# A first MLP product by seven block products: a linear-attention and MLP kernel on one Trainium2 core

## The chip, the cores and the metric

The kernel runs on one core of a Trainium2 chip. The metric is the device time in microseconds of one execution; a time is given as the median of several runs. Lower is better. The engines are named as in the profile: PE is TensorE's matmul stream and PEld its weight loads, DVE is VectorE, ACT is ScalarE, POOL is GpSimd, SP is SyncE, whose queue issues most DMAs.

## The reference

A gated linear attention (batch 4, 8 heads, 768 tokens, head dimension 48) feeds a two-layer MLP with an ELU between the layers (3072 tokens, model dimension 384, hidden dimension 2048).

```python
f = 1.0 / (1.0 + np.exp(-f_logit))
for t in range(S):
    state = f[:, :, t, :, None] * state + np.einsum('bhd,bhe->bhde', k[:, :, t], v[:, :, t])
    y[:, :, t] = np.einsum('bhd,bhde->bhe', q[:, :, t], state)
x = y.transpose(0, 2, 1, 3).reshape(B * S, H * D)
h = x @ w_in
g = np.where(h > 0.0, h, np.exp(np.minimum(h, 0.0)) - 1.0)
out = g @ w_out
```

All tensors that the kernel computes with are fp32. The weights arrive in a wider type and are converted at the start.

## The kernel before

The 3072 tokens are cut into 12 units of 256 tokens (`NU`, `U`). For every unit the kernel runs the attention, which leaves the unit's MLP input in a tile `xt` with channels on the partitions: three channel tiles of 128 (`NKT`), and a fourth (`HP` is 4) that is only a source from which six small DMAs fill the remaining rows (L699). The MLP of a unit is cut into eight block pairs j of 256 hidden channels (`NP`). A pair P = (unit m, j) goes through these stages:

- `up(P)`: the first product, h = w_in-block transposed times `xt`, as two halves of 128 hidden channels by 256 tokens in one PSUM bank (tag `h`, two banks). Each half is three matmuls of 256 columns, one for each channel tile (L780). ScalarE then computes Relu(-h) and Exp of its negative (L785, L786).
- `elu(P)`: VectorE joins both to the ELU (L792), and for units from 2 on (`DIRECT`) forms four sums of 128x128 blocks of it (L802).
- `down(P)`: the second product. For units 0 and 1 it is four matmuls of 384 columns (L813). From unit 2 on it already is a product by seven block products of 192 columns (L835), in the manner of Strassen and Winograd: the sums of `elu` and four combinations of the w_out blocks (`combos`, made by `combine`) take the place of the eighth. After the last pair of a unit ScalarE and VectorE put the output together from four PSUM banks (L845, L846).

The attention of a unit runs in pieces: `load` (DMAs of q, k, f and v), `gates` (four ScalarE instructions and small GpSimd ones), `decays` four times (a scan and a reciprocal on VectorE at L576 and L579, products with k and q on GpSimd at L580 and L583), `transposed` (TensorE transposes, L598), `advance` (state updates on TensorE, L650), `step` (two VectorE instructions for each of four chunks, L613 and L616), `scores` and `mask` (L629, L637), `outputs` (L666) and `carried` (L686, then the copies into `xt`, L693 and L695, and the six DMAs).

The order on every engine is the order in which the code is written, under a manual schedule. The main loop counts steps T: at an even T it issues `up(T/2)`, at an odd one `down` of the pair two before (`LAG`), and ahead of them whatever `at_step` has planned for T. The attention of unit u is planned around t = (u-1)*16, one unit ahead of its MLP: `load` at t-16, `gates` at t-8, the four `decays` at t-6 to t, and the rest at t+2 to t+10. `reread` and `check` bring the weights in once more and reduce them to their smallest and largest magnitude on VectorE (L551); `finish_flag` turns this and the gates' range (`watch`) into a flag. If the flag is bad, a slower general version runs afterwards; it does not run here.

Of the kernel before, what the change touches and what calls it, by code (L numbers as in the profile page):

```python
# [8 lines left out]
FP32 = mybir.dt.float32  # L9
# [347 lines left out]
def fast(ctx: ExitStack, tc: tile.TileContext, q, k, v, f_logit, w_in, w_out, out, flag):  # L357
# [11 lines left out]

    nc = tc.nc
    B, H, D, S = q.shape
    DM = H * D
# [14 lines left out]
    DIRECT = 2  # L389
    LAG = 2  # L390
    AHEAD = 7
    LIMIT = 2.0**60
    HALF = (slice(0, D), slice(64, 64 + D))
    FULL = (slice(0, 64), slice(64, 128))
# [3 lines left out]
    sb = ctx.enter_context(tc.tile_pool(name="sb", bufs=2))  # L398
    ps = ctx.enter_context(tc.tile_pool(name="ps", bufs=1, space=bass.MemoryType.PSUM))

    NB = 3
    qkf = [{n: cst.tile([128, HP, U], FP32, name=f"{n}{i}") for n in "fqk"} for i in range(NB)]
    src = {"q": q, "k": k, "f": f_logit}
    vs = [cst.tile([128, NW, DM + PAD], FP32, name=f"v{i}") for i in range(NB)]
# [66 lines left out]
        area[:, 0:4].bitcast(FP32).rearrange("p a f -> p (a f)").rearrange("p (c n f) -> p c n f", c=4, f=DH)  # L471
    )


    both = (0, 1, 2, 3, 4, 5, 8, 9, 10, 6, 11, 7, 12, 13, 14, 15)
    order = [divmod(i, NP) for i in both] + [(m, j) for m in range(2, NU) for j in range(NP)]
# [58 lines left out]

    spans = cst.tile([128, 2, NFT], FP32, name="spans")

    def reread(n):  # L540

        if wide:
            flat = (w_out if n % 2 else w_in).rearrange("a b -> (a b)").rearrange("(p i f) -> i p f", p=128, f=2 * DM)
            nc.sync.dma_start(out=area[:, 4 + n % (AHEAD - 4)], in_=flat[n // 2])

    def check(n):

        if not wide:
            return
        for i, op in enumerate((ALU.min, ALU.max)):  # L550
            nc.vector.tensor_reduce(  # L551
                out=spans[:, i, n : n + 1], in_=area[:, 4 + n % (AHEAD - 4)].bitcast(FP32)[:, 1::2],
                axis=mybir.AxisListType.X, op=op, apply_absolute_value=True,
            )

    def gates(u, pieces=(2, 2)):
# [118 lines left out]
    def carried(u):  # L675

        t = qkf[u % NB]
        py = pys.pop(u)
        for w in range(NW):
            for p in range(HP):  # L680
                for b in range(2):
                    c = 2 * w + b
                    if (u % UPB, c) == (0, 0):
                        continue
                    for r in range(2):
                        nc.tensor.matmul(  # L686
                            py[b][HALF[r ^ b], w, p], lhsT=sts[u, c][HALF[r], p],
                            rhs=t["q"][HALF[r], p, c * C : (c + 1) * C],
                            start=False, stop=True, skip_group_check=True,
                        )  # L690
        x = xts[u] = sb.tile([128, HP, U], FP32, tag="xt", name=f"xt{u}", bufs=3)
        to = x[:].rearrange("n p (w b i) -> n b w p i", b=2, i=C)
        nc.scalar.copy(to[:, 0], py[0][:])  # L693
        for r in range(2):
            nc.scalar.copy(to[FULL[r], 1], py[1][FULL[1 - r]])  # L695
        for i in range(2 * NKT):
            r, j = divmod(i, NKT)
            frm, g = 64 * r + j * PAD, 64 * r + D
            nc.sync.dma_start(out=x[g : g + PAD, j, :], in_=x[frm : frm + PAD, NKT, :])  # L699

    def first_outputs(part):


        q_, at = qkf[0]["q"], ats[0]
        for gap in range(2):
            for w in range(NW):
                for p in range(NKT):
                    for r in range(2):
                        h = 2 * p + r
                        for b in range(2):  # L710
                            c = 2 * w + b
                            if part and c == 0:
                                continue
                            pair = NKT if gap else p
                            if part:
                                lhs = padded_s[HALF[r], c - 1, p] if gap else sts[0, c][HALF[r], p]
# [13 lines left out]
        if part == 0:  # L730
            for b in range(2):
                nc.scalar.copy(between[:, :, 0:NKT], first_y[b][:, :, :, 0])
            return
        x = xts[0] = sb.tile([128, HP, U], FP32, tag="xt", name="xt0", bufs=3)
# [7 lines left out]
    def at_step(step, *todo):  # L742
        plan.setdefault(step, []).extend(todo)

    def attention(u, first, then):

        kept = []
        for p, i in enumerate(first):
            at_step(i, lambda p=p: decays(u, p))
        if first:  # L750
            at_step(first[-1], lambda: watch(u))
        at_step(then[0], lambda: transposed(u, 0, "a0"), lambda: transposed(u, 1, "a1"))
        at_step(then[1], lambda: advance(u), *(lambda c=c: step(u, c) for c in range(NC)))
        at_step(then[2], lambda: kept.append(scores(u)))
        at_step(then[2], lambda: mask(u, kept[0]))
        at_step(then[3], lambda: outputs(u))
        at_step(then[4], lambda: carried(u))

    gs, ss, pms, phs = {}, {}, {}, {}

    def combine():
# [3 lines left out]
        for n in range(0, NP, 2):  # L765
            for to, x, y in (
# [4 lines left out]
                )  # L771
                yield

    def up(P):

        m, j = order[P]
        ph = ps.tile([128, 2, U], FP32, tag="h", name=f"psH{m}_{j}", bufs=2)
        for i in range(2):
            for kt in range(NKT):
                nc.tensor.matmul(  # L780
                    ph[:, i], lhsT=wi[j][:, kt, i * 128 : (i + 1) * 128], rhs=xts[m][:, kt, :],
                    start=(kt == 0), stop=(kt == NKT - 1),
                )
        g = gs[P] = sb.tile([128, 2, U], FP32, tag="gg", name=f"gg{m}_{j}", bufs=4)
        nc.scalar.activation(g[:], ph[:], AF.Relu, scale=-1.0)  # L785
        nc.scalar.activation(g[:], g[:], AF.Exp, scale=-1.0)  # L786
        phs[P] = ph

    def elu(P):
        m, j = order[P]  # L790
        g = gs[P]
        nc.vector.scalar_tensor_tensor(  # L792
            out=g[:], in0=g[:], scalar=-1.0, in1=phs.pop(P)[:], op0=ALU.add, op1=ALU.max
        )
        if m >= DIRECT:
            s = ss[P] = sb.tile([128, 4, 128], FP32, tag="sums", name=f"sums{m}_{j}", bufs=3)
            a = [[g[:, i, t * 128 : (t + 1) * 128] for i in range(2)] for t in range(2)]
            for i, x, y, op in (
                (0, a[1][0], a[1][1], ALU.add), (2, a[0][0], a[1][0], ALU.subtract),
                (1, s[:, 0], a[0][0], ALU.subtract), (3, a[0][1], s[:, 1], ALU.subtract),  # L800
            ):
                nc.vector.tensor_tensor(out=s[:, i], in0=x, in1=y, op=op)  # L802

    def down(P):
        m, j = order[P]
# [51 lines left out]
                    )  # L857
            del pms[m]

    def finish_flag():  # L860
        if wide:
# [7 lines left out]
        low = cst.tile([128, 1], FP32, name="low")  # L869
        nc.vector.tensor_reduce(  # L870
            out=low[:], in_=fine[:].rearrange("p a c -> p (a c)"), axis=mybir.AxisListType.X, op=ALU.min
        )
# [51 lines left out]
    decays(1, 1)  # L924
    step(0, NC - 1)
    watch(0)
    blank(2, nc.gpsimd)
    at_step(0, lambda: decays(1, 2))
    at_step(1, lambda: decays(1, 3), lambda: watch(1))
    at_step(4, lambda: warm(4))  # L930
    attention(1, (), (2, 4, 5, 6, 7))
    for n in range(1, NFT):
        t = max(needs[n][0] - 2, 0)
        at_step(t, lambda n=n: merge(n))
# [4 lines left out]
    attention(2, (14, 16, 18, 20), (22, 24, 26, 27, 28))  # L939
    weights = combine()  # L940
    for n in range(NFT):
        at_step(28 + n, lambda: next(weights))
    for u in range(3, NU):
        t = (u - 1) * NFT
        at_step(t - 16, lambda u=u: load(u))
        at_step(t - 8, lambda u=u: gates(u))
        attention(u, (t - 6, t - 4, t - 2, t), (t + 2, t + 4, t + 6, t + 8, t + 10))
    for n in range(NFT):
        t = (3 + n) * NFT + 9 if n < 7 else (NU - 2) * NFT + 9 + 2 * (n - 7) if n < 10 else (NU - 1) * NFT + 2 * n - 20
        at_step(t - 6, lambda n=n: reread(n))  # L950
        at_step(t, lambda n=n: check(n))
    at_step((NU - 1) * NFT + 13, lambda: finish_flag())
    for T in range(NU * NFT):
        P = T // 2
        if T % 2 == 0 and P:
            elu(P - 1)
        for f in plan.pop(T, ()):
            f()
# [54 lines left out]
```

## Time and profile before

| | before |
|---|---|
| median of 9 runs | 587.11 us (585.44 to 590.57) |
| the profiled execution | 586.22 us |
| its span, first to last instruction | 584.4 us |
| granted TensorE clock | 0.988 |
| PE busy / matmul instructions | 567.8 us / 5596 |
| DVE busy | 398.1 us |
| ACT busy | 217.6 us |
| POOL busy | 79.0 us |
| DMA traffic | 50.81 MB, mean 87 GB/s |

The profile is of one execution. A "busy" time is the union of an engine's instructions; their mean duration can be longer than their spacing, because matmuls are pipelined. An fp32 matmul of the program shows as two MATMUL and two LDWEIGHTS records. Groups are given as line, engine, operation, output and inputs, shape and count, then busy time and the mean duration in ns. Timeline rows give start and length in microseconds, then the same fields.

### The profile page before, as it was taken

To read this page: it belongs to the slowest core of one execution; us is meant where nothing else is said; L and a number is where in the kernel's file an instruction comes from. 1 tells how busy PE (TensorE), PEld (TensorE's weight loads), DVE (VectorE), ACT (ScalarE), POOL (GpSimd) and SP (SyncE) were. 2 spreads that over 40 slices of the span, in tenths; PEclk is the share of its full clock that TensorE was granted. 3 is DMA by queue.
4 is the path that set the end of the run, shared out by engine and by line. 5 is a ranking of instruction groups with operands and counts; after the bars stand their busy time and mean duration, and the time that the engine had idled before them with its cause. 6 is when DMAs were issued, how large, how long until landed. Compare 5 with 4: busy or idle time off the path is not lost.

```text
span 584.4 us, 13417 instructions
## 1 busy us (share of the span) xinstructions
PE 567.8 (97%) x5596; PEld 492.9 (84%) x5596; DVE 398.1 (68%) x806; ACT 217.6 (37%) x357; POOL 79.0 (14%) x161
## 2 busy tenths in 40 slices
PE   7699999999999999999999999999999999999995
PEld 2467777777899999999999899999899999999995
DVE  7899667666586676576676776766766767665852
ACT  3367845433433332432433333243252242232221
POOL 6350021020020020020021011011011011000000
PEclk9889999999999999999999999999999999999998
DMA  8999880061071061051042043034024010305401
GB/s 189 237 221 273 182 206 0 2 124 47 2 161 33 6 157 38 4 117 63 21 94 82 22 77 95 29 61 110 29 52 118 29 45 19 136 17 208 136 2 33
DMA packets 34823, 50.81 MB, mean 87 GB/s; under 512 B 4000, under 2 KB 27584, under 8 KB 34752
## 3 DMA queue, kind: packets, MB, share of 16 engines
q1 hardware_dynamic: 33840, 49.07, 33.6%
q8 instruction: 46, 0.75, 0.6%
q10 hardware_dynamic: 912, 0.79, 0.5%
q14 instruction: 25, 0.20, 0.1%
HBM read 44.04 MB, written 4.72 MB: 83 GB/s over the span
## 4 chain that ended last, share of the span: by engine, by line
PE 95%; issue 1%; POOL 1%; DMA 1%; ACT 1%; DVE 0%; DVEq 0%; POOLq 0%; ACTq 0%
PE psH L780 44%; PE psM L835 31%; PE psM L813 7%; PE psS L629 2%; PE psY L666 2%; PE psU_a L650 2%; PE psY L686 2%; PE psW L881 2%; PE psT L598 2%; PE psY L725 1%; DMA f<-in_f_logit_dram 1%; POOL k L580 0%; ACT f L564 0%; DVE at L637 0%; ACT f L563 0%
## 5 line engine op out<-in xcount | busy, mean ns | idle before, releaser
L780 PE MATMUL psH<-xt,wi 128*128 128x256 f32 x1152 | 269.3, 383 | 0.0
L780 PEld LDWEIGHTS psH<-xt,wi 128*128 128x128 f32 x1152 | 214.2, 190 | 31.4 <-issue 1.0
L785 ACT ACTIVATE gg<-psH 128x512 f32<-128x512 f32 x96 | 57.5, 599 | 268.8 <-PE psH L780 268.6
L792 DVE SCALAR_TENSOR_TENSOR gg<-gg,psH 128x512 f32<-128x512 f32 x96 | 65.8, 685 | 109.4 <-ACT gg L786 109.3
L835 PE MATMUL psM<-area,sums 128*128 128x192 f32 x480 | 91.1, 326 | 0.0
L579 DVE RECIPROCAL p<-f 128x256 f32<-128x256 f32 x48 | 84.1, 1753 | 1.7
L835 PEld LDWEIGHTS psM<-area,sums 128*128 128x128 f32 x480 | 80.2, 190 | 0.0
L835 PE MATMUL psM<-wo,gg 128*128 128x192 f32 x320 | 65.2, 326 | 0.0
L786 ACT ACTIVATE gg<-gg 128x512 f32<-128x512 f32 x96 | 60.5, 630 | 3.1
L835 PEld LDWEIGHTS psM<-wo,gg 128*128 128x128 f32 x320 | 56.3, 190 | 4.0
L580 POOL TENSOR_TENSOR k<-k,f 128x256 f32<-128x256 f32 x48 | 35.5, 741 | 166.5 <-DVE f L576 163.3
L813 PE MATMUL psM<-wo,gg 128*128 128x384 f32 x128 | 44.2, 488 | 0.0
L802 DVE TENSOR_TENSOR sums<-gg 128x128 f32<-128x128 f32 x160 | 39.4, 287 | 2.8
L835 PE MATMUL psM<-area,gg 128*128 128x192 f32 x160 | 39.1, 326 | 0.0
L835 PE MATMUL psM<-wo,sums 128*128 128x192 f32 x160 | 39.1, 326 | 0.0
L845 DVE TENSOR_TENSOR o<-psM,u 128x192 f32<-128x192 f32 (+1 forms) x30 | 11.8, 420 | 38.4 <-ACT u L846 38.1
L566 POOL COPY restart<-f 128x8 f32<-128x8 f32 (+1 forms) x24 | 4.8, 200 | 243.8 <-ACT f L564 240.2
L813 PEld LDWEIGHTS psM<-wo,gg 128*128 128x128 f32 x128 | 24.1, 190 | 13.6
L525 ACT ACTIVATE area<-area 128x768 uint16<-128x768 uint32 x16 | 30.4, 1934 | 4.7 <-DVE area L519 2.3
L576 DVE TENSOR_TENSOR_SCAN f<-f,restart 128x256 f32<-128x256 f32 x47 | 31.9, 680 | 0.0
L551 DVE TENSOR_REDUCE spans<-area 128x1 f32<-128x768 f32 x32 | 28.9, 944 | 0.0
L835 PEld LDWEIGHTS psM<-area,gg 128*128 128x128 f32 x160 | 28.2, 190 | 0.0
(82 smaller groups left out, 461.9 us busy)
## 6 DMA issues: line engine op xcount, KB each, us to landing
area<-in_moe_w_out_dram SPq DMA_DIRECT2D x16, 768.0 KB, 7.3
area<-in_moe_w_in_dram SPq DMA_DIRECT2D x8, 768.0 KB, 6.5
v<-in_v_dram SPq DMA_DIRECT2D x12, 384.0 KB, 6.8
area<-in_moe_w_in_dram SPq DMA_DIRECT2D x16, 288.0 KB, 8.3
f<-in_f_logit_dram SPq DMA_DIRECT2D x23, 192.0 KB, 3.8
k<-in_k_dram SPq DMA_DIRECT2D x23, 192.0 KB, 4.9
q<-in_q_dram SPq DMA_DIRECT2D x23, 192.0 KB, 6.0
out_dram<-o SPq DMA_DIRECT2D x38, 96.0 KB, 1.7
```

The source lines that it names most:

```text
L525: nc.scalar.activation(raw.bitcast(U16)[:, 2::4], raw.bitcast(U32)[:, 0::2], AF.Copy, scale=2.0**-29)
L551: nc.vector.tensor_reduce(out=spans[:, i, n : n + 1], in_=area[:, 4 + n % (AHEAD - 4)].bitcast(FP32)[:, 1::2], axis=mybir.AxisListType.X, ...
L576: nc.vector.tensor_tensor_scan(out=a, data0=a, data1=restart[:, p] if u or p else a, initial=1.0, op0=ALU.mult, op1=ALU.max)
L579: nc.vector.reciprocal(pts[u][:, p], g)
L580: nc.gpsimd.tensor_tensor(out=t["k"][:, p], in0=t["k"][:, p], in1=g, op=ALU.mult)
L780: nc.tensor.matmul(ph[:, i], lhsT=wi[j][:, kt, i * 128 : (i + 1) * 128], rhs=xts[m][:, kt, :], start=(kt == 0), stop=(kt == NKT - 1),)
L785: nc.scalar.activation(g[:], ph[:], AF.Relu, scale=-1.0)
L786: nc.scalar.activation(g[:], g[:], AF.Exp, scale=-1.0)
L792: nc.vector.scalar_tensor_tensor(out=g[:], in0=g[:], scalar=-1.0, in1=phs.pop(P)[:], op0=ALU.add, op1=ALU.max)
L802: nc.vector.tensor_tensor(out=s[:, i], in0=x, in1=y, op=op)
L813: nc.tensor.matmul(pm[t][:], lhsT=g[:, i, t * 128 : (t + 1) * 128], rhs=wo[:, 2 * j + i, :], start=(j == 0 and i == 0), stop=(j == NP - 1 ...
L835: nc.tensor.matmul(pm[bank][:, half * DH : (half + 1) * DH], lhsT=x, rhs=y, start=first, stop=(j == NP - 1), skip_group_check=True,)
```

## The change

From unit 2 on the first product is also computed by block products. Over the first two channel tiles, two 128-channel halves and two 128-token halves, seven products of 128x128 blocks replace eight; the third channel tile is added into three of them by matmuls into the same PSUM blocks. This takes ten matmuls, nine of 128 columns and one of 256, in two PSUM banks `pa` and `pb` of the tag `h`. Block combinations of w_in are made once on GpSimd (`mix`, in the part of `area` that the weights no longer use), those of `xt` once a unit on GpSimd (`blend`), with `xt` one tile longer. ScalarE copies one block (`u1`), VectorE adds the blocks into an SBUF tile `hh` (`up7`, `joined`), and ScalarE's two passes then read `hh` (`exped`). The four sums of `elu` move from VectorE to GpSimd, and `elu(P-1)` is issued between the two halves of `up7(P)`.

Around this, the attention's pieces get new steps (`A1`, `D2`, `A2`, `D3`, `A3`), `step` gets a slot of its own behind `advance`, q, k, f and v have two buffers instead of three (one blanking goes), the weights are reread in 32 smaller pieces into the tile `bits`, four steps apart from unit 3 to unit 10, and `finish_flag` is split in two.

```diff
+    A1 = (2, 4, 4, 5, 6, 7)
+    D2 = (14, 16, 18, 20)
+    A2 = (22, 24, 24, 26, 27, 28)
+    D3 = (-7, -5, -3, -1)
+    A3 = (2, 4, 5, 7, 9, 11)
+    BL = 13
+    RR = 0
+    MX = 21
...
-    NB = 3
+    NB = 2
...
+    mixes = cst.tile([128, NP, 4, 128], FP32, name="mixes") if not wide else (
+        area[:, 4:7].bitcast(FP32).rearrange("p a f -> p (a f)")[:, 0 : NP * 512]
+        .rearrange("p (n c f) -> p n c f", n=NP, c=4)
+    )
...
-            flat = (w_out if n % 2 else w_in).rearrange("a b -> (a b)").rearrange("(p i f) -> i p f", p=128, f=2 * DM)
-            nc.sync.dma_start(out=area[:, 4 + n % (AHEAD - 4)], in_=flat[n // 2])
+            flat = (w_out if n % 2 else w_in).rearrange("a b -> (a b)").rearrange("(p i f) -> i p f", p=128, f=DM)
+            again[n] = sb.tile([128, 2 * DM], I32, tag="bits", name=f"again{n}")
+            nc.sync.dma_start(out=again[n][:].bitcast(w_in.dtype), in_=flat[n // 2])
...
-        x = xts[u] = sb.tile([128, HP, U], FP32, tag="xt", name=f"xt{u}", bufs=3)
+        x = xts[u] = sb.tile([128, HP + 1, U], FP32, tag="xt", name=f"xt{u}", bufs=3)
...
-        at_step(then[1], lambda: advance(u), *(lambda c=c: step(u, c) for c in range(NC)))
-        at_step(then[2], lambda: kept.append(scores(u)))
-        at_step(then[2], lambda: mask(u, kept[0]))
-        at_step(then[3], lambda: outputs(u))
-        at_step(then[4], lambda: carried(u))
+        at_step(then[1], lambda: advance(u))
+        at_step(then[2], *(lambda c=c: step(u, c) for c in range(NC)))
+        at_step(then[3], lambda: kept.append(scores(u)), lambda: mask(u, kept[0]))
+        at_step(then[4], lambda: outputs(u))
+        at_step(then[5], lambda: carried(u))
...
+    def mix(j):
+        a = [[wi[j][:, k, i * 128 : (i + 1) * 128] for k in range(2)] for i in range(2)]
+        t = [mixes[:, j, i] for i in range(4)]
+        for to, x, y, op in (
+            (t[0], a[1][0], a[1][1], ALU.add), (t[1], t[0], a[0][0], ALU.subtract),
+            (t[2], a[0][0], a[1][0], ALU.subtract), (t[3], a[0][1], t[1], ALU.subtract),
+        ):
+            nc.gpsimd.tensor_tensor(out=to, in0=x, in1=y, op=op)
+
+    def blend(u):
+        x = xts[u][:].rearrange("n k (t i) -> n (k t) i", t=2)
+        for to, a, b in ((7, 3, 1), (1, 1, 0), (8, 3, 1), (9, 2, 8), (6, 4, 5)):
+            nc.gpsimd.tensor_tensor(out=x[:, to], in0=x[:, a], in1=x[:, b], op=ALU.subtract)
+
+    def up7(P):
+        m, j = order[P]
+        x = xts[m][:].rearrange("n k (t i) -> n (k t) i", t=2)
+        a = [[wi[j][:, k, i * 128 : (i + 1) * 128] for k in range(3)] for i in range(2)]
+        t = [mixes[:, j, i] for i in range(4)]
+        pa, pb = (ps.tile([128, 4, 128], FP32, tag="h", name=f"psH{m}_{j}_{i}", bufs=2) for i in range(2))
+
+        def products(*todo):
+            for n, (to, lhs, rhs) in enumerate(todo):
+                nc.tensor.matmul(to, lhsT=lhs, rhs=rhs, start=(n == 0), stop=True, skip_group_check=True)
+
+        products(
+            (pa[:, 0], a[0][0], x[:, 0]), (pa[:, 1], t[1], x[:, 8]), (pa[:, 2], a[0][1], x[:, 2]),
+            (pa[:, 2], a[0][2], x[:, 4]),
+        )
+        u1 = sb.tile([128, 128], FP32, tag="u1", name=f"u1_{m}_{j}")
+        nc.scalar.copy(u1[:], pa[:, 0])
+        h = sb.tile([128, 5, 128], FP32, tag="hh", name=f"hh{m}_{j}")
+        add = lambda to, x, y: nc.vector.tensor_tensor(out=to, in0=x, in1=y, op=ALU.add)
+        add(h[:, 0:2], pa[:, 1:3], u1[:].unsqueeze(1).broadcast_to([128, 2, 128]))
+        if order[P - 1][0] >= DIRECT:
+            elu(P - 1)
+        products(
+            (pb[:, 0], t[0], x[:, 1]), (pb[:, 2], t[2], x[:, 7]), (pb[:, 3], a[1][1], x[:, 9]),
+            (pb[:, 2:4], a[1][2], x[:, 5:7]), (pb[:, 1], t[3], x[:, 3]), (pb[:, 1], a[0][2], x[:, 5]),
+        )
+        phs[P] = h, pb
+
+    def joined(P):
+        m, j = order[P]
+        h, pb = phs[P]
+        add = lambda to, x, y: nc.vector.tensor_tensor(out=to, in0=x, in1=y, op=ALU.add)
+        u43 = sb.tile([128, 2, 128], FP32, tag="u43h", name=f"u43h{m}_{j}")
+        add(u43[:], pb[:, 0::2], h[:, 0:1].broadcast_to([128, 2, 128]))
+        add(h[:, 2:4], pb[:, 1::2], u43[:])
+        add(h[:, 4], pb[:, 0], u43[:, 1])
+        exped(P, h[:, 1:].rearrange("n (i t) f -> n i (t f)", i=2))
...
+        if m >= DIRECT:
+            up7(P)
+            return
...
-                nc.vector.tensor_tensor(out=s[:, i], in0=x, in1=y, op=op)
+                nc.gpsimd.tensor_tensor(out=s[:, i], in0=x, in1=y, op=op)
...
-    blank(2, nc.gpsimd)
...
+    for j in range(NP):
+        at_step(MX + j, lambda j=j: mix(j))
+    at_step(30, lambda: blend(2))
     for u in range(3, NU):
         t = (u - 1) * NFT
+        at_step(t + BL, lambda u=u: blend(u))
         at_step(t - 16, lambda u=u: load(u))
         at_step(t - 8, lambda u=u: gates(u))
-        attention(u, (t - 6, t - 4, t - 2, t), (t + 2, t + 4, t + 6, t + 8, t + 10))
-    for n in range(NFT):
-        t = (3 + n) * NFT + 9 if n < 7 else (NU - 2) * NFT + 9 + 2 * (n - 7) if n < 10 else (NU - 1) * NFT + 2 * n - 20
-        at_step(t - 6, lambda n=n: reread(n))
-        at_step(t, lambda n=n: check(n))
-    at_step((NU - 1) * NFT + 13, lambda: finish_flag())
+        attention(u, [t + i for i in D3], [t + i for i in A3])
+    for n in range(NR):
+        t = 3 * NFT + (NU - 4) * NFT * n // NR + RR
+        at_step(t, lambda n=n: reread(n))
+        at_step(t + 4, lambda n=n: check(n))
+    at_step((NU - 1) * NFT + 9, lambda: finish_flag(0))
+    at_step((NU - 1) * NFT + 13, lambda: finish_flag(1))
     for T in range(NU * NFT):
         P = T // 2
-        if T % 2 == 0 and P:
+        sevens = order[P][0] >= DIRECT
+        if T % 2 and sevens:
+            joined(P)
+        if T % 2 == 0 and P and order[P - 1][0] < DIRECT:
             elu(P - 1)
```

`exped(P, h)` holds the two ScalarE passes that stood at the end of `up(P)`. In units 0 and 1 `up`, `elu` and `down` stay as they were.

More of the change, by code (lines that the diff above doesn't have):

```diff
@@ L534, in merge @@
         fetch(n + AHEAD)
-    spans = cst.tile([128, 2, NFT], FP32, name="spans")
+    NR = 2 * NFT
+    spans = cst.tile([128, 2, NR], FP32, name="spans")
+    again = {}
     def reread(n):
         if wide:
-            flat = (w_out if n % 2 else w_in).rearrange("a b -> (a b)").rearrange("(p i f) -> i p f", p=128, f=2 * DM)
-            nc.sync.dma_start(out=area[:, 4 + n % (AHEAD - 4)], in_=flat[n // 2])
+            flat = (w_out if n % 2 else w_in).rearrange("a b -> (a b)").rearrange("(p i f) -> i p f", p=128, f=DM)
+            again[n] = sb.tile([128, 2 * DM], I32, tag="bits", name=f"again{n}")
+            nc.sync.dma_start(out=again[n][:].bitcast(w_in.dtype), in_=flat[n // 2])
     def check(n):
@@ L549, in check @@
             return
+        hi = again.pop(n)[:].bitcast(FP32)[:, 1::2]
         for i, op in enumerate((ALU.min, ALU.max)):
             nc.vector.tensor_reduce(
-                out=spans[:, i, n : n + 1], in_=area[:, 4 + n % (AHEAD - 4)].bitcast(FP32)[:, 1::2],
-                axis=mybir.AxisListType.X, op=op, apply_absolute_value=True,
+                out=spans[:, i, n : n + 1], in_=hi, axis=mybir.AxisListType.X, op=op, apply_absolute_value=True
             )
@@ L690, in carried @@
                         )
[L691 to L692 removed]
+        x = xts[u] = sb.tile([128, HP + 1, U], FP32, tag="xt", name=f"xt{u}", bufs=3)
+        to = x[:, 0:HP].rearrange("n p (w b i) -> n b w p i", b=2, i=C)
         nc.scalar.copy(to[:, 0], py[0][:])
@@ L733, in first_outputs @@
             return
-        x = xts[0] = sb.tile([128, HP, U], FP32, tag="xt", name="xt0", bufs=3)
+        x = xts[0] = sb.tile([128, HP + 1, U], FP32, tag="xt", name="xt0", bufs=3)
         to = x[:, 0:NKT].rearrange("n p (w b i) -> n b w p i", b=2, i=C)
@@ new lines, in joined, with exped @@
+    def joined(P):
[7 more added lines that the diff above has]
+        exped(P, h[:, 1:].rearrange("n (i t) f -> n i (t f)", i=2))
+    def exped(P, h):
+        m, j = order[P]
+        g = gs[P] = sb.tile([128, 2, U], FP32, tag="gg", name=f"gg{m}_{j}", bufs=4)
+        nc.scalar.activation(g[:], h, AF.Relu, scale=-1.0)
+        nc.scalar.activation(g[:], g[:], AF.Exp, scale=-1.0)
+        phs[P] = h
@@ L783, in up @@
                 )
[L784 to L787, printed above, removed]
+        exped(P, ph[:])
     def elu(P):
@@ L792, in elu @@
         nc.vector.scalar_tensor_tensor(
-            out=g[:], in0=g[:], scalar=-1.0, in1=phs.pop(P)[:], op0=ALU.add, op1=ALU.max
+            out=g[:], in0=g[:], scalar=-1.0, in1=phs.pop(P), op0=ALU.add, op1=ALU.max
         )
@@ L858, in down, with finish_flag @@
             del pms[m]
-    def finish_flag():
-        if wide:
+    low = cst.tile([128, 1], FP32, name="low")
+    def finish_flag(part):
+        if wide and not part:
             ok = fine[:, 0, 0:1]
@@ L868, in finish_flag @@
                 )
[L869 to L872, printed above, removed]
+        if not part:
+            nc.vector.tensor_reduce(
+                out=low[:], in_=fine[:].rearrange("p a c -> p (a c)"), axis=mybir.AxisListType.X, op=ALU.min
+            )
+            return
         pf = ps.tile([128, 1], FP32, tag="a0", name="psF")
@@ L930, in fast @@
     at_step(4, lambda: warm(4))
-    attention(1, (), (2, 4, 5, 6, 7))
+    attention(1, (), A1)
     for n in range(1, NFT):
@@ L938, in fast @@
     at_step(12, lambda: gates(2))
-    attention(2, (14, 16, 18, 20), (22, 24, 26, 27, 28))
+    attention(2, D2, A2)
     weights = combine()
```

## The prediction

> **What bounds the kernel now.** I read the page first, then the chain of waits in a late unit, then the PE timeline and the weight loads, and last DVE and GpSimd in the same unit.
>
> ```profile
> PE 567.8 (97%) x5596; PEld 492.9 (84%) x5596; DVE 398.1 (68%) x806; ACT 217.6 (37%) x357; POOL 79.0 (14%) x161
> ```
>
> TensorE is busy 97% of the span. In the chain over 354 to 400 us nothing but TensorE appears:
>
> ```profile
> 354.16 2.59 PE psH L780 x12
> 356.75 2.27 PE psM L835 x14
> 359.02 0.87 PE psT L598 x8
> ```
>
> A block pair P costs 2.59 us for the first product (twelve passes: six matmuls, each fp32 matmul recorded as two), 2.27 for the second, and a unit of eight pairs with its attention 44.89 (the stretch below). No wait of TensorE shows there, so time is won only by shortening its stream, and lost when a new wait enters it. What a shorter pass costs:
>
> ```profile
> 353.99 2.75 PE L780 MATMUL psH<-xt,wi 128*128 128x256 f32 x12
> 358.86 1.04 PE L598 MATMUL psT<-ident,k 128*128 128x128 f32 x8
> 364.69 1.15 PE L650 MATMUL psU_a<-v,kn 64*64 64x48 f32 x64
> 370.83 1.16 PE L629 MATMUL psS<-q,k 48*64 48x64 f32 x64
> 383.14 1.11 PE L686 MATMUL psY<-q,state 48*48 48x64 f32 x64
> ```
> ```profile
> L780 PEld LDWEIGHTS psH<-xt,wi 128*128 128x128 f32 x1152 | 214.2, 190 | 31.4 <-issue 1.0 <-DVE gg L792 0.6
> L629 PEld LDWEIGHTS psS<-q,k 48*64 48x64 f32 x768 | 12.5, 134 | 4.1 <-issue 3.2 <-PE psH L780 0.7 <-DVE bits L515 0.2
> L598 PEld LDWEIGHTS psT<-ident,k 128*128 128x128 f32 x96 | 11.2, 141 | 4.1 <-POOL k L580 2.6 <-issue 0.9
> ```
>
> The reader is to see the spacing: first line, (2.75 - 0.38)/11 = 0.216 us per 256-column pass; transposes, (1.04 - 0.27)/7 = 0.109 per 128 columns, but with a load of only 141 ns instead of 190. 192 columns take 2.27/14 = 0.162. So columns cost 0.84 ns each, as long as the next weight load hides. The three packed lines run four tiles at once: per four, (1.15 - 0.22)/63 x 4 = 59 ns with 48 columns streamed and 64 loaded; 60 with 64 and 64; 57 with 64 streamed and 48 loaded. The load sets the first two.
>
> The other engines in that unit, and the one place where GpSimd meets a VectorE instruction with two SBUF inputs:
>
> ```profile
> 353.99:398.88 44.89, 44.89 (x474) 41.22 (x473) 30.30 (x66) 15.51 (x28) 5.58 (x11) 1.00 0.27 64
> ```
> ```profile
> 33.68 0.95 DVE L533 CUSTOM_DVE_ANT_0 wi<-area,bits 128x1536 uint16<-128x1536 uint16 x1
> 33.70 1.51 POOL L583 TENSOR_TENSOR q<-q,p 128x256 f32<-128x256 f32 x1
> ```
>
> **The change, part by part.**
>
> *First product (80 pairs).* Removed: 12 passes of 256 columns, 2.59 us. Added: nine matmuls of 128 columns and one of 256, so 18 short passes and 2 long ones (1408 columns instead of 1536; Strassen spares only two of three channel tiles). At the transposes' 0.109 that is 18 x 0.109 + 0.43 = 2.39. But here every pass has a full fp32 load under it. A load of 64 columns lasts 134 ns, of 128, 190: 56 more. Added to the load-bound 58 ns (the packed step without its exposed first load) that is 0.114. I take 0.112, between: 18 x 0.112 + 0.43 = 2.45, **0.14 us less per pair, 11.4 us in 80**. Ends: 16 us at 0.109, 9 at 0.114. The break-even is (2.59 - 0.43)/18 = 0.120: eight nanoseconds decide the sign.
>
> A rule speaks against it. The Trainium skill, "TensorE: Matmul & The Clock Gate", section "Back-to-back issue gap", says that in a stream of load-and-multiply pairs both set the spacing: about 81 ns at 128 columns where the isolated gap is about 56 (bf16). Those 25 ns on our 0.109 would give 0.134, 2.84 us per pair, 20 us slower in all. No row here shows that loss: the transposes pay none, the packed tiles 2 to 3 ns. I go by the rows, and keep the rule as a rival.
>
> *VectorE.* The four sums leave (0.29 each, about 1.0 together because they overlap). Four adds come: 128x192 from PSUM takes 0.36 and 128x384 0.55 (L845), so 128x256 about 0.42 three times, 128x128 0.29 once: 1.55. With the ELU's 0.69 a pair needs 2.2, or 2.0 with the overlap seen in the sums (two in 0.49); 2.0 taken. The range check becomes 32 pairs of half-width reduces, four a unit: 0.94 us at 768 columns, so about 0.5 each, 4 us a unit against some 2. Unit total: 30.3 - 8 + 12.4 + 2 = 37 of 43.7, or 84%: no bound on average.
>
> *Where it is tight.* With up(P) at 0, the first bank is done at 0.9, its add can start at 1.45 (drain, ScalarE's copy, about 0.25 by the 0.30 that L846 takes for 192 columns, semaphores); the second bank is drained at 2.6, joined to 3.7. Its bank is wanted again at 4.72 + 0.9 = 5.6: 1.9 us to spare. The loop join, two ScalarE passes (0.63 each), ELU, next join is about 3.2, under the period of 4.72. In the four pairs with decays VectorE also has scan 0.68 (L576) and reciprocal 1.75 (L579): 4 x (2.0 + 2.43) + two checks 2.0 + product and watch 0.6 = 20.3 against 4 x 4.72 = 18.9, 1.4 late. The gates (four ScalarE instructions of 0.63, L563 and L564) now sit ahead of a bank copy: 0.9 more. So 2.3 late where the next join may be about 3 late (the transposes, 1 us, come before that bank). Late first would be the second bank. **I take 0.25 us in each of nine units, +2.3**; ends 0 and 2 us a unit (18).
>
> *GpSimd.* Takes 4 sums a pair. Between the 128x128 affine select's 0.29 and the 128x256 product's 0.73; half of the columns at the product's slope, 0.41, so 1.6 us a pair (1.2 to 2.9). ELU(P) ends near 7.3, its sums near 9; the down product needs them at 11.8 + 0.6. Even 2.9 hides. Five blend subtractions per unit (2.1) follow carried's three ScalarE copies (1.8) and six DMAs on SP (3.8, landing 1.8), some 11 us after it starts; its unit begins 13 after. Sums queued behind the blend wait less than their slack. The 32 mixes (13 us) fall into steps 21 to 28, when POOL is almost idle. For unit 2 xt lands near 125 us, blended at 127.4, needed at 128.96: +0.3 taken, ends 0 and 2.
>
> A second rule: "SBUF — State Buffer", section "Who interferes with whom": a VectorE instruction with two SBUF inputs and a GpSimd one that reads SBUF exclude each other for their whole length. The trace agrees: 1.51 us instead of 0.73 beside L533. Otherwise, in the steady units, GpSimd overlaps only the reciprocal (one input), so they don't show what comes: joins read PSUM and pass, but a scan right after a join can meet the last sum. By the rows alone 0; by the rule up to 0.41 in each of four scans, 1.6 us a unit. It is why I take 0.25 above rather than nothing, and most of that price's upper end.
>
> *Moved or costing nothing.* Carried, outputs and scores move by up to two steps; their matmuls and the four exposed loads a unit (0.1 us each) stay. State steps (eight VectorE, 2.9 us) leave advance's slot for the next; pairs there have over 2 us free. Two q/k/f buffers instead of three: a load must wait for carried two units earlier, but SP already holds it behind that unit's xt copies, and the gates come half a unit later. 32 rereads instead of 16: 16 more SP issues of 0.45; each needs the check placed four steps earlier. The dropped blanking frees 2.9 us of POOL before TensorE's stream. All hidden by TensorE's 4.7 us pairs; uncovered, a reread or late load would hold SP's queue, and with it the xt copies.
>
> *Tail.* Last join 1.1, ScalarE 1.3, ELU 0.7, three sums 1.2, handoffs 0.5: 4.8 after the last up, against two downs and two products, 5.2. +0.3 taken, ends 0 and 1.
>
> **Sum.** -11.4 + 2.3 + 0.3 + 0.3 = -8.5. The profiled execution took 586.22 (584.4 span and 1.8 around), so it becomes 577.7; the median 587.11 stands 0.9 above it: **578.6**.
>
> **Rivals.** (1) *The weight load does not hide.* At 0.134 a pass: 607 us; slower from 0.120. For it: the rule, and a 190 ns load under a 109 ns pass occurs nowhere in this trace. Against: the packed tiles, load-bound at only 5 ns above what their columns need. 0.15. (2) *VectorE, late in the decay pairs, gives it back.* 1.0 to 1.6 us lost in each of nine units: 585 to 590, about 587. For: 84% load, the shared port. Against: the transposes' slack. 0.15. (3) *Everything hides and passes run at 0.109:* 571; for it the transposes' line; against, their shorter load. It is the low end of my case.
>
> **How the numbers follow.** My case with (3), 570.5 to 583.5: 0.70, all faster by over 0.5%, about what a measurement of this kernel can tell from no change. Rival (2): 0.02 faster, 0.07 within, 0.06 slower. Rival (1): 0.15 slower. Faster 0.72, same 0.07, slower 0.21. The range runs from 570.5 to 590, through rival (2), and leaves out rival (1) alone.
>
> **What would show it.** Passes of 128 columns 109 to 114 ns apart, 20 per up; a pair at 4.6 to 4.8 us; TensorE still 96% or more; VectorE 80 to 88%, POOL about 40%. Wrong if short passes start over 120 ns apart, or if waits of psH matmuls for VectorE's adds, or of psM matmuls for GpSimd's sums, add up to over 10 us.

## The result, and the profile after

The changed kernel takes 579.58 us (median of 10 runs, 576.15 to 582.2) against 586.69 (median of 31 runs, 584.68 to 594.69). The ratio is 0.9868, 95% interval 0.9843 to 0.9894: 7.7 us faster by the ratio, where 8.5 was forecast; the median is 579.58 where 578.6 was. The profiled execution took 581.5 us, 579.8 of it the span, so it is among the slower ones. Of one version below, two runs at a lower granted clock than the others are left out.

First the page of the changed kernel, busy times and two groups of the new first product (mean duration in ns after the comma):

```profile
PE 557.4 (96%) x6236; PEld 506.0 (87%) x6236; DVE 437.4 (75%) x838; ACT 235.5 (41%) x437; POOL 270.8 (47%) x559
...
L819 PE MATMUL psH<-xt,area 128*128 128x128 f32 x640 | 110.6, 275 | 0.0
L819 PEld LDWEIGHTS psH<-xt,area 128*128 128x128 f32 x640 | 96.8, 192 | 4.1
```

TensorE stays the bound at 96%. VectorE went from 68% to 75% of the span, GpSimd from 14% to 47%. Then a pair in the chain of waits, and short passes in the timeline:

```profile
441.70 2.44 PE psH L819 x20
444.14 2.28 PE psM L916 x14
446.42 0.87 PE psT L616 x8
```
```profile
447.58 0.61 PE L819 MATMUL psH<-xt,wi 128*128 128x128 f32 x4
448.02 0.61 PE L819 MATMUL psH<-xt,area 128*128 128x128 f32 x4
```

The first product fell from 2.59 to 2.44 us. The spacing is read as before: (0.61 - 0.275)/3 = 0.112 us per 128-column pass, with a load of 192 ns under each. Of all short passes from unit 2 on that another short or long pass follows, nearly all start 109 to 113 ns before it, most 111 or 112.

The engines in one unit (PE, PEld, DVE, ACT, POOL busy, then clock, DMA share and rate):

```profile
353.55:397.54 43.99, 43.76 (x537) 42.41 (x537) 36.10 (x72) 17.20 (x37) 24.76 (x51) 1.00 0.35 87
```

A unit fell from 44.89 to 43.99 us. Over units 3 to 10 it is 43.77 to 44.29, mean 43.99. VectorE is busy 36.1 of 44.0 us, 82%. TensorE's waits from 175 to 560 us, units 3 to 11 (total us, times, longest), are one row:

```profile
PE psS L647 <- DVE state L631: 0.7, 3, 0.3
```

**Where the time went.** From the start of unit 2's first product to the end, the two profiles take 455.4 and 446.4 us: 9.0 less. Eighty pairs, the plain ones 4.715 instead of 4.865 us long and the others shorter by as much, give 12.0. In eight units the pair that holds the scores takes 6.08 to 6.60 us where 6.0 is the least that later runs show: 2.4 us given back. The tail takes about 0.5 more. Ahead of unit 2 these two profiles differ by 4.4 us the other way: it starts at 133.4 us in this one and at 129.0 in the one before. With that only 4.6 us of span are left between them. The medians' 7.7 fit a start that is later by 1.3 us or so; this is inferred, for only one execution of each was traced (more on the start at the end).

The chain of waits through the pair with the scores in unit 9, the costliest one, shows what TensorE waited for:

```profile
454.64 0.82 DVE o L926 x2
455.46 0.92 DVE spans L570 x2
456.39 0.33 DVE hh L828
...
457.24 0.43 DVE u43h L841
457.68 0.62 DVE hh L841 x2
458.31 0.28 DVE state L631
...
460.56 0.37 DVE state L631
460.97 1.16 PE psS L647 x62
```

TensorE drops out of the chain for ten microseconds (it works on meanwhile, at what is ready). VectorE runs the output sums of the unit before, then a range check of 1 us, then the bank add, the ELU, the join and the state steps one after another. Only when the last sum of the state steps (L631) has read its bank may the scores write into it. The pair is 0.6 us longer for it, and 0.1 to 0.55 us in the other seven.

### The profile page after: what moved, and what is told of

Same layout as the page of the kernel before. It is cut to its first block, busy times and chain, and to the rows that moved or that the text cites. A ratio compares the mean times of both kernels' runs of the same rounds, so it can differ in the third digit from the quotient of the medians.

```text
span 579.8 us, 15424 instructions
## 1 busy us (share of the span) xinstructions
PE 557.4 (96%) x6236; PEld 506.0 (87%) x6236; DVE 437.4 (75%) x838; ACT 235.5 (41%) x437; POOL 270.8 (47%) x559
## 4 chain that ended last, share of the span: by engine, by line
PE 87%; DVE 5%; DMA 4%; ACT 1%; issue 1%; POOL 1%; DVEq 0%; POOLq 0%; ACTq 0%
PE psH L819 32%; PE psM L916 31%; PE psH L864 7%; PE psM L894 7%; PE psS L647 2%; PE psY L684 2%; PE psY L704 2%; DMA area<-in_moe_w_in_dram 2%; PE psU_a L668 2%; PE psT L616 2%; DMA k<-in_k_dram 1%; DMA f<-in_f_logit_dram 1%; DVE state L631 1%; DVE p L597 1%; PE psW L965 1%
## 5 line engine op out<-in xcount | busy, mean ns | idle before, releaser
L819 PE MATMUL psH<-xt,wi 128*128 128x128 f32 (+1 forms) x960 | 177.1, 293 | 0.0
L883 POOL TENSOR_TENSOR sums<-gg 128x128 f32<-128x128 f32 x160 | 69.7, 456 | 180.6 <-DVE gg L873 136.1
L851 ACT ACTIVATE gg<-hh 128x512 f32<-128x512 f32 x80 | 50.4, 631 | 224.1 <-POOL sums L883 131.0
L819 PEld LDWEIGHTS psH<-xt,wi 128*128 128x128 f32 x960 | 135.9, 192 | 0.8
L819 PE MATMUL psH<-xt,area 128*128 128x128 f32 x640 | 110.6, 275 | 0.0
L819 PEld LDWEIGHTS psH<-xt,area 128*128 128x128 f32 x640 | 96.8, 192 | 4.1
L828 DVE TENSOR_TENSOR hh<-psH,u 128x256 f32<-128x256 f32 x80 | 33.6, 420 | 68.8 <-ACT u L826 68.8
L873 DVE SCALAR_TENSOR_TENSOR gg<-gg,hh 128x512 f32<-128x512 f32 x80 | 56.7, 708 | 1.5 <-ACT gg L852 1.5
L841 DVE TENSOR_TENSOR hh<-psH,u43h 128x256 f32<-128x256 f32 (+1 forms) x160 | 49.6, 352 | 2.7
L864 PE MATMUL psH<-xt,wi 128*128 128x256 f32 x192 | 46.3, 393 | 0.5 <-DMA xt<-xt 0.5
L883 POOL TENSOR_TENSOR sums<-gg,sums 128x128 f32<-128x128 f32 x80 | 43.4, 543 | 6.3
L864 PEld LDWEIGHTS psH<-xt,wi 128*128 128x128 f32 x192 | 37.0, 196 | 8.3 <-DVE gg L873 1.1
L841 DVE TENSOR_TENSOR u43h<-psH,hh 128x256 f32<-128x256 f32 x80 | 33.5, 419 | 7.5 <-PE psH L819 7.5
```

What stands on the lines that cost most here:

```text
L819: nc.tensor.matmul(to, lhsT=lhs, rhs=rhs, start=(n == 0), stop=True, skip_group_check=True)
L828: add = lambda to, x, y: nc.vector.tensor_tensor(out=to, in0=x, in1=y, op=ALU.add)
L841: add = lambda to, x, y: nc.vector.tensor_tensor(out=to, in0=x, in1=y, op=ALU.add)
L851: nc.scalar.activation(g[:], h, AF.Relu, scale=-1.0)
L864: nc.tensor.matmul(ph[:, i], lhsT=wi[j][:, kt, i * 128 : (i + 1) * 128], rhs=xts[m][:, kt, :], start=(kt == 0), stop=(kt == NKT - 1),)
L873: nc.vector.scalar_tensor_tensor(out=g[:], in0=g[:], scalar=-1.0, in1=phs.pop(P), op0=ALU.add, op1=ALU.max)
```

## The experiments

All ratios are to the kernel before, measured on the same chip.

**The price of a short pass alone.** The kernel before, with each 256-column matmul cut in two.

```diff
-            for kt in range(NKT):
-                nc.tensor.matmul(
-                    ph[:, i], lhsT=wi[j][:, kt, i * 128 : (i + 1) * 128], rhs=xts[m][:, kt, :],
+            for h in (slice(0, 128), slice(128, 256)):
+                for kt in range(NKT):
+                    nc.tensor.matmul(
+                        ph[:, i, h], lhsT=wi[j][:, kt, i * 128 : (i + 1) * 128], rhs=xts[m][:, kt, h],
...
```

> The kernel before with every 256-column matmul of the first product cut into two of 128 columns, the same block loaded for each, nothing else. It measures the price of a 128-column pass with a full fp32 load under it. My theory: passes 0.112 us apart, 24 of them in a pair, 2.69 us instead of 2.59, 0.10 x 96 pairs = 9 us slower, about 596 us. The rival that the load does not hide (0.134): 3.22 us a pair, 60 us slower, about 647. If passes run at the transposes' 0.109: 2 us slower, 589.

Measured: 596.62 us, ratio 1.0183 (1.0136 to 1.023). Its timeline of TensorE:

```profile
304.18 2.84 PE L781 MATMUL psH<-xt,wi 128*128 128x128 f32 x24
306.86 0.82 PE L836 MATMUL psM<-wo,gg 128*128 128x192 f32 x4
```

From the first to the next product 306.86 - 304.18 = 2.68 us for 24 passes, 0.112 each. The full load under a pass of its own width costs at most some 3 ns (0.112 against the 0.109 of the transposes, whose load is shorter). The rival of 0.134 is out.

**The first product put back, all else kept.** `up7`, `joined`, `mix` and `blend` taken out; the new steps, two buffers, the 32 rereads and the sums on GpSimd stay.

```diff
-        if m >= DIRECT:
-            up7(P)
-            return
...
-        if T % 2 and sevens:
-            joined(P)
-        if T % 2 == 0 and P and order[P - 1][0] < DIRECT:
+        if T % 2 == 0 and P:
             elu(P - 1)
```

> The changed kernel with its first product put back to six matmuls of 256 columns; the new steps of the attention, two buffers, the reread in 32 pieces and the sums on GpSimd stay. My theory (the time comes from TensorE's shorter stream alone): the whole gain goes, 586 to 587 us, pairs at 4.87 us. Rival (the gain, or a part of it, comes from the new order, the lighter VectorE or the dropped blanking): 580 to 584.

Measured: 588.22 us, ratio 1.0017 (0.9994 to 1.004). The whole gain is gone, and every unit from 3 to 10 is back at 44.88 or 44.89 us. The order, the buffers and the sums' move are worth nothing by themselves. What the sums' move and one of the new steps are worth to the shorter stream, the runs that take them back show below.

**The sums back on VectorE.**

```diff
-                nc.gpsimd.tensor_tensor(out=s[:, i], in0=x, in1=y, op=op)
+                nc.vector.tensor_tensor(out=s[:, i], in0=x, in1=y, op=op)
```

> The changed kernel with the four sums back on VectorE. My theory: VectorE gets about 0.95 us a pair, 7.6 a unit, on top of some 37 to 38, so it needs 45 us a unit and becomes the bound, or nearly: units 45 to 46 us, 10 to 18 us slower than the changed kernel, waits of TensorE for VectorE in the decay pairs. Rival (GpSimd's port costs as much as it takes over, so the move is neutral): within 3 us of the changed kernel.

Measured: 639.63 us, ratio 1.0877 (1.0809 to 1.0944). The direction was right, the size far off: I expected 45 to 46 us a unit, and they take 49.5 to 51.5. TensorE's waits, and one unit (columns as above):

```profile
PE psH L819 <- DVE hh L841: 40.3, 31, 1.8
PE psS L647 <- DVE state L631: 1.4, 3, 0.5
```
```profile
334.26:385.71 51.45, 45.69 (x537) 42.98 (x537) 44.07 (x106) 16.79 (x36) 8.16 (x16) 1.00 0.31 73
```

The matmuls wait for the join's reads (L841): the second bank, as the prediction named it. VectorE is busy only 44.1 of 51.5 us. My sum of its work was about right, but I treated it as an average. With one bank of slack (1.9 us by the prediction's sum) VectorE can't carry the surplus of the heavy pairs over to the light ones: 6.3 of its 7.4 idle us in this unit fall into three pairs, and over all units most of its waiting is for ScalarE's copy of the first bank (41.2 us in 21 waits). The run changes VectorE's load and its order at once, as the sums now stand ahead of the join; it does not tell the two apart.

**No range check.** The rereads and their reduces are left out, so the flag rests on the gates' range alone.

```diff
+    nc.vector.memset(spans[:], 1.0)
...
-    for n in range(NR):
-        t = 3 * NFT + (NU - 4) * NFT * n // NR + RR
-        at_step(t, lambda n=n: reread(n))
-        at_step(t + 4, lambda n=n: check(n))
```

> The changed kernel without the reread of the weights and its range reduces (the flag then rests on the gates' range alone). My theory: TensorE's remaining waits sit where scores wait for VectorE's state steps, which are late because a check (1.0 us) and the output sums stand ahead of them; without the checks they vanish, units fall from 44.0 on average to 43.8, 2 to 3 us faster in all. Rival (the waits have another cause, the order of the pieces or GpSimd): units stay at 44.0 and the time within 1 us.

Measured: 577.22 us, ratio 0.9833 (0.9785 to 0.9881). The scores' pair takes 6.0 us in every unit, and seven of the eight units 43.68 to 43.70. One took 44.3; there a down product waited 0.6 us for GpSimd's sums, once.

**The checks two steps later,** so that none stands ahead of the state steps.

```diff
-    RR = 0
+    RR = 2
```

> The changed kernel with RR = 2: every reread and check two steps later, so that no check falls on step t+4, ahead of the state steps that the scores wait for. My theory (scores wait for state steps, delayed by that check): the scores' pair falls from 6.1 to 6.6 us to 6.0, units to 43.7 to 43.8, 2 us faster than the changed kernel, some 577 us. Rival (it is VectorE's total load, wherever the check stands): the wait moves to another pair and units stay at 44.0.

Measured: 577.10 us, ratio 0.9829 (0.9806 to 0.9853). Its chain at the same place holds nothing but TensorE:

```profile
455.70 2.44 PE psH L819 x20
458.14 1.09 PE psS L647 x64
459.23 2.47 PE psM L916 x14
```

All checks are still there, and the wait is gone: units 43.68 to 43.85, 444.1 us from unit 2 to the end instead of 446.4. So it was the place of one check and not VectorE's load. The totals' intervals overlap with those of the changed kernel; the 2.3 us are shown by the unit times, not by the totals.

**The same, with the very last pair's sums on VectorE.**

```diff
+                (nc.vector if P == NU * NP - 1 else nc.gpsimd).tensor_tensor(out=s[:, i], in0=x, in1=y, op=op)
```

> As the version with the checks two steps later, and in addition the sums of the very last pair on VectorE, where nothing else is left to do. My theory: 2 us from the scores' wait and 0.3 to 0.8 from a shorter tail, 576 to 577 us. Rival (the tail is set by the output's DMAs): no difference from the version with the later checks.

Measured: 577.19 us, ratio 0.9829 (0.9803 to 0.9856): no difference from the version above. The tail was not waiting for those sums.

**The state steps a slot earlier,** where they stood before the change.

```diff
-    A3 = (2, 4, 5, 7, 9, 11)
+    A3 = (2, 4, 4, 7, 9, 11)
```

> The changed kernel with the state steps issued with advance at t+4 again, as before the change, instead of at t+5. My theory: the steps (3 us on VectorE) now stand ahead of the first bank's add and the ELU of that pair; the scores no longer wait for them, but the add, the join and so the second bank come up to 3 us later, where 1.9 are to be had: 0.5 to 1.5 us a unit lost there, 4 to 12 us slower than the changed kernel. Rival (the slot does not matter): within 1 us of the changed kernel.

Measured: 596.97 and 603.59 us, with no interval to give: 1.8 and 2.9% slower than the kernel before. In the profiled run (603.59) three of the units 3 to 10 take 45.6 to 46.2 us, some 1.9 more than in the changed kernel, where 0.5 to 1.5 was expected. The other five take 47.6 to 48.1. TensorE's waits:

```profile
PE psH L819 <- DVE hh L828: 11.2, 8, 1.9
PE psH L819 <- DVE hh L841: 4.2, 8, 0.5
```

The waits are for the `h` banks, as expected, but mainly for the first one (L828), where the expectation had named the second. They are 15.4 us in eight units, 1.9 in each: steps, output sums and check now stand together ahead of one bank add.

The rest of the loss in the five long units is the clock. Unit 5, behind the wait (columns as above), and TensorE's rows there:

```profile
288.60:292.00 3.40, 3.40 (x24) 3.00 (x28) 1.25 (x3) 1.24 (x3) 1.55 (x5) 0.50 0.12 47
...
289.39 1.49 PE L819 MATMUL psH<-xt,wi 128*128 128x128 f32 x4
290.67 0.64 PE L819 MATMUL psH<-xt,area 128*128 128x128 f32 x2
```

The granted clock is 0.50 for 3.4 us in each of the five, and 1.00 throughout the three others. The four passes at 289.39 take 1.28 us to the next start; in the pair before, at full clock, the same four took 0.65. So of the 3.6 to 4.1 us lost in these units some 1.7 (half of 3.4, an estimate) go to the clock. Each stretch begins behind a wait of this kind (1.9 to 2.4 us in the unit), but the three others wait 1.2 to 2.0 us without one, and with the sums on VectorE some 5 us of waits a unit brought none. What sets it off stays open.

**GpSimd's load nearly doubled.** Four additions that nothing uses follow the sums.

```diff
+            for i in range(4):
+                nc.gpsimd.tensor_tensor(out=twin[:, i], in0=g[:, i // 2, 0:128], in1=g[:, i % 2, 128:256], op=ALU.add)
...
+    twin = cst.tile([128, 4, 128], FP32, name="twin")
```

> The changed kernel with four more GpSimd additions a pair that nothing uses, after the four sums: GpSimd's load nearly twice as large, VectorE's and TensorE's work the same. My theory (GpSimd has room, and the shared port costs VectorE a little): GpSimd about 85% in the units, VectorE 2 to 3 us a unit longer by the port, units 44.3 to 45.0, 3 to 9 us slower than the changed kernel. Rival (GpSimd is already close to the limit): down products wait for sums, over 2 us a unit, 16 us or more slower. If the port cost nothing and GpSimd had room: no difference.

Measured: 589.65 us, ratio 1.0051 (1.0031 to 1.0071), some 11 us slower than the changed kernel by the ratios. Units take 44.5 to 46.2, where 44.3 to 45.0 was expected. VectorE's busy time rose little, to 37.6 and 36.4 us in units 6 and 7; the 2 to 3 us a unit that were expected from the shared port did not come. TensorE's waits:

```profile
PEld psT L616 <- POOL k L598: 7.3, 8, 1.0
PEld psM L918 <- POOL sums L883: 5.0, 6, 1.4
PE psM L918 <- POOL sums L883: 3.0, 4, 1.1
```

With 38 of 45 us, GpSimd is late: transposes wait for its product with k, down products for sums. So at 24 us a unit GpSimd had room, and at 38 it has none left. That lies between my theory and the rival, nearer to the theory in the time.

**The start of the run.** The next three ask why unit 2 starts later in the seven-product kernels. The traces settle two things first. The difference arises ahead of unit 1: from its start to that of unit 2 both kernels take 47.33 us. And a part of it is the clock. The same stretch, before and after (columns as above):

```profile
41.20:44.60 3.40, 3.40 (x43) 1.47 (x42) 2.63 (x5) 3.37 (x6) 0.00 (x0) 1.00 1.08 183
...
41.20:44.60 3.40, 3.40 (x10) 2.69 (x9) 3.33 (x7) 1.38 (x2) 0.20 (x1) 0.51 1.07 227
```

Both kernels have 10.2 us at half the granted clock near 25 us; the changed one has these 3.4 us more. That is at most 1.7 us of its 4.4 (half of 3.4, an estimate). Three of the six other profiles of seven-product kernels with the fallback have such an additional stretch; the three without it start unit 2 at 131.0 to 133.0 us, still 2 us or more late.

The general version written twice in the branch of the kernel before:

```diff
             general(tc, q, k, v, f_logit, w_in, w_out, out)
+            general(tc, q, k, v, f_logit, w_in, w_out, out)
```

> In all profiles so far the first 20 us bring in 3.6 to 3.8 MB with the seven-product kernels and 4.07 to 4.14 with the three others, and their unit 2 starts some 3 us later. What is executed in those 20 us is the same. This is the kernel before with the general version written twice in the branch that does not run: a larger program, nothing else. Theory A (the size or placement of the program in memory slows the first loads): 3.6 to 3.8 MB in 20 us, unit 2 starting at 131 to 134 us, 2 to 3 us slower than before. Theory B (it is the layout of SBUF): as before, 4.1 MB, 129 us, no difference. Theory C (chance): either.

Measured: 589.8 us, ratio 1.0071 (1.0047 to 1.0096), for code that does not run. 3.97 MB in the first 20 us, unit 2 at 132.3 us, units unchanged at 44.89, and 1.7 us more in the tail. This trace has an additional half-clock stretch too (3.4 us at 52.3), so up to 1.7 of its 3.3 us at the start may be the clock.

The changed kernel without the branch:

```diff
-        with tc.If(seen < 128):
-            general(tc, q, k, v, f_logit, w_in, w_out, out)
```

> The changed kernel without the branch that does not run (the general version is left out; the flag is still computed and read). Theory A (size or placement of the program): 4.0 to 4.15 MB in the first 20 us, unit 2 starts near 130 us, 2 to 3 us faster than the changed kernel, about 577 us. Theory B (SBUF layout): 3.6 to 3.8 MB, no difference.

Measured: 577.39 us, ratio 0.9884 (0.9841 to 0.9927): no gain over the changed kernel by the ratio, though its one trace comes close to theory A: 3.98 MB in 20 us, no additional half-clock stretch, unit 2 at 129.8 us. That trace is of the fastest of its four runs (575.06 to 580.56 us).

The trace shows one thing more. The program ends 3.2 us after VectorE's last addition, the changed kernel 6.0 after it, the kernel before 5.5, the one with two fallbacks 7.1. The DMA queues of the changed kernel in its last 6.0 us have these rows (packets, MB, share), and the end of the one without the branch has none of their kind:

```profile
q14 instruction: 7, 0.06, 3.5%
q8 instruction: 1, 0.02, 1.1%
```

So a branch that is not taken goes with instruction loads at the end and some 2.8 us more there, in this one pair of traces.

The version with the plain first product, with the working tiles of the seven products laid out again:

```diff
+    def spare():
+        for tag, n in (("hh", 640), ("u1", 128), ("u43h", 256)):
+            for i in range(2):
+                nc.gpsimd.memset(sb.tile([128, n], FP32, tag=tag, name=f"{tag}_{i}")[:], 0.0)
+    at_step(40, spare)
```

> The version with the plain first product (six matmuls of 256 columns), with the three working tiles of the seven products (hh, u1, u43h) laid out in SBUF again and written once by GpSimd at step 40, used for nothing. Theory B (SBUF layout): 3.6 to 3.8 MB in the first 20 us, unit 2 starts at 131 us or later. Theory A (program): 4.1 MB, about 129.7 us.

Measured once: 588.07 us, 4.32 MB in 20 us, unit 2 at 130.9 us, with an additional half-clock stretch (3.4 us at 71.3). The layout with these tiles did not slow the first loads. That the program's size or place in memory slows the start is suggested by the first of the three and by the second's trace, and not borne out by the second's ratio. Beyond the clock's part the cause stays open.

## Why the prediction was right, point by point

- **TensorE's passes.** Forecast 0.112 us from two neighbouring rows, measured 0.112, in the changed kernel and in the kernel before with split passes. The 11.4 us became 12.0, because the short passes are 0.1114 us apart on average: a product takes 2.44 us instead of my sum of 2.45, and 80 pairs multiply the rounding.
- **The rule on spacing** (the Trainium skill, "TensorE: Matmul & The Clock Gate", "Back-to-back issue gap") did not carry over: its extra 25 ns at 128 columns is 3 ns for these fp32 passes. Had I gone by it, I would have forecast 20 us slower.
- **VectorE's lateness.** Forecast +2.3 us, measured 2.4, for the wrong reason; that the two agree is luck. I put it in the decay pairs, at the second bank. There TensorE never waited in the changed kernel; 1.9 us and the transposes' microsecond were enough. It came at the scores, behind the state steps, of which I had written that their pairs have over 2 us free. I had not put the output sums (2.2 us) and the check (1.0), which run ahead of the steps, into that account. That is the step that failed; the later check shows it.
- **VectorE's and GpSimd's load.** 37 us a unit forecast, 36.1 measured. A GpSimd sum takes 0.46 us in the median, against 0.41 taken, and up to 0.87; with 1.9 us a pair it stays hidden. GpSimd is busy 47% of the span, where about 40 was forecast.
- **The shared port** (the Trainium skill, "SBUF — State Buffer", "Who interferes with whom") is seen in the changed kernel, and costs nothing where it falls. A scan before the change; then, in the changed kernel, a scan that meets a sum, and the end of unit 8:

```profile
439.77 0.68 DVE L576 TENSOR_TENSOR_SCAN f<-f,restart 128x256 f32<-128x256 f32 x1
...
424.82 0.68 DVE L594 TENSOR_TENSOR_SCAN f<-f,restart 128x256 f32<-128x256 f32 x1
424.88 0.87 POOL L883 TENSOR_TENSOR sums<-sums,gg 128x128 f32<-128x128 f32 x1
...
440.46 1.01 DVE L594 TENSOR_TENSOR_SCAN f<-f,restart 128x256 f32<-128x256 f32 x1
440.89 1.11 POOL L601 TENSOR_TENSOR q<-q,p 128x256 f32<-128x256 f32 x1
...
443.64 0.43 DVE L606 SCALAR_TENSOR_TENSOR fine<-f,fine 128x16 f32<-128x16 f32 x1
```

At 424.8 the scan comes first and keeps its 0.68 us, and the sum takes 0.87 instead of 0.46. At 440 the scan takes 1.01, GpSimd's product with q 1.11 instead of 0.73, and the small watch later 0.43 instead of 0.17. With the sums back on VectorE every scan from unit 3 on is at 0.68 again and the watch at 0.17. So the meetings come with the work that GpSimd took over: some scans meet its sums, others its products, which now come later. It is up to 0.59 us in one scan, more than the 0.41 I allowed, but 0.3 to 0.7 us a unit over the four scans, where I had put down up to 1.6. In the version with later checks scans still reach 1.27 us, and TensorE's matmuls show no wait at all.

- **The start and the tail.** 0.3 each forecast, and neither came as named. Unit 2's first pair waits for no blend and no mix. The last addition comes 44.18 us after the start of unit 11 instead of 45.38, the full gain of eight pairs; the 0.5 us that the tail takes longer lie behind it. What the start does ahead of unit 1 was not in the sum: six other profiles of seven-product kernels with the fallback in place start unit 2 at 131.0 to 135.2 us, the kernel before and the changed one with the plain product put back at 129.0 and 129.7.
- **The rivals.** VectorE late and the gain given back was near: with the steps a slot earlier, or the sums on VectorE, the same change is 2 to 9% slower than the kernel before.

## What to carry to other kernels

Cost a narrower matmul by the spacing of the starts in rows of its own type, not by the durations shown: here fp32 passes of 128 columns start 0.112 us apart, though a pass shows 275 ns and its load 192. Halving 256 columns loses under 4% (2.68 us against 2.59), so that a scheme with fewer columns pays, if barely. Before adding work to an engine that issues in a fixed order, sum up its queue between two handoffs, all planned pieces included, not over the whole unit: at 82% of the unit VectorE still held TensorE up in one pair, and a two-step move of a check that nobody waits for took that away. The best version here that keeps every check is that one, 577.10 us, ratio 0.9829.

## What was not expected of the hardware

After each stretch of packed 48- or 64-row matmuls the first full matmul takes some 103 ns longer, four times a unit: 483 instead of 379 ns before the change (256 columns), 377 instead of 275 after it (128 columns) and 430 instead of 326 (192). Its weight load starts with it and not ahead of it, as in the changed kernel behind the state updates:

```profile
453.02 0.30 PEld L819 LDWEIGHTS psH<-xt,wi 128*128 128x128 f32 x2
453.02 0.49 PE L819 MATMUL psH<-xt,wi 128*128 128x128 f32 x2
```

Code that never runs moved the time by 0.7% (ratio 1.0071, interval 1.0047 to 1.0096): with a second copy of the fallback the first loads and the tail were slower in its trace, with the units in between at their old times. Taking the fallback out of the changed kernel brought nothing that the totals show, though its trace has a shorter end. Differences of half a percent between programs of different size are to be read from the unit times, not from the total alone.

With the state steps a slot earlier, five of eight units had 3.4 us at a granted clock of 0.50 behind waits of about 2 us. The loss of a version is then not its wait alone, and the granted clock in a short stretch tells the two apart.
